# Warming products, the order of two GpSimd products and the places of weight loads in a fused attention and mixture-of-experts kernel

## The chip, the cores and the metric

The kernel runs on one core of one Trainium2 chip. The metric is the device time of one execution in microseconds (us); the time before the change is 430.35 us, the median of three runs (429.88 to 430.53). The engines are called TensorE (PE in the profile; PEld is its loading of weights), VectorE (DVE), ScalarE (ACT), GpSimd (POOL) and SyncE (SP, which here only issues transfers). "L351" is line 351 of the kernel before.

## The reference

Three stages run one after the other on 2 sequences of 768 tokens, all in fp32.

```python
for t in range(S):                       # 1: attention with a decaying state, 8 heads of 64
    state = gamma * state + outer(k[:, :, t], v[:, :, t])
    y[:, :, t] = scale * q[:, :, t] @ state
# 2: every token goes to one of 8 experts
e = argmax(x @ w_gate), or the expert of the token before, where sigmoid(x @ w_local) >= 0.5
out = softmax(x @ w_gate)[e] * (relu(x @ w1[e]) @ w2[e])         # 512 -> 1024 -> 512
# 3: a gated layer
h = relu(x @ w_in); gate = sigmoid(conv over 3 tokens of h); out = (h * gate) @ w_out
```

The weights of the third stage arrive as 64-bit floats, which the kernel decodes itself.

## The kernel before, in words

**The attention** is cut into 12 tiles of 128 tokens. A loop over i = 0 to 11 does tile i's second half and tile i+1's first half, so that the engines overlap. All instructions go into their engine's queue in the order in which the code writes them, and each engine works in that order; there is no scheduler.

- `a_S(i)` (L344): 16 products k by q on TensorE (L351), then VectorE masks them into A (L357, two instructions).
- `a_Z(i)` (L360): 16 products of q with the state carried over (L367).
- `a_AV(i)` (L371): 16 products of v with A (L379), the first eight on heads 0 to 3 and the others on heads 4 to 7; then ScalarE copies the result to xT (L384).
- `a_U(i)` (L387): 16 products that add k by v to the state (L397), and ScalarE's copy Z of it (L399).
- `a_X(i)` (L401): 8 products that turn xT into rows and give the gate's logits (L407); ScalarE copies the rows (L417) and stores them to DRAM (`a_store`, L410).
- `a_scale_q(i, engine)` (L324): q times a table of decays (L330). On GpSimd a one-element memset comes first (L328). It overwrites an element of the tile before, so it waits for that tile's products `a_S`.
- `a_scale_v(i)` (L332): v times its decays, heads 4 to 7 by one GpSimd instruction (L337), heads 0 to 3 by four on ScalarE (L340).
- `a_table(c)` (L318): ScalarE makes the tables of decays, one in each of the first steps.

The loop's step i issues `a_Z(i)`, the load of q and k for tile i+3, `a_X(i-1)`, `a_AV(i)`, `a_U(i)`, the load of k and v for tile i+3, `a_S(i+1)`, then `a_scale_q(i+2)` on GpSimd and `a_scale_v(i+1)`. Between these stand the pieces of the routing (`route`, L444, a generator advanced by `part`): after tiles 3, 6, 9, 11 and 12 a group of tiles gets its experts, its counts and its slots, in short VectorE instructions with small TensorE products between them. In step 8 `first_gather` (L590) reads the first expert's first 128 slots out of the state's PSUM bank (L594, L595) before `a_U(8)` may write that bank again, and GpSimd gathers those rows.

**Weights.** Each expert has 8 pieces of 512 KB (four of w1, four of w2), numbered over all experts in their order of use; I call them unit 0, unit 1, and so on. `load_unit` (L152) issues the next one on SP, into one of four buffers. `split_first` (L168) makes a unit's high part on ScalarE (L174), `split_second` (L178) its low part on VectorE (L183), which frees the buffer and then, unless told not to, loads another unit. Products use high and low parts in three passes. `LOADS` says how many loads stand at the end of each step of the attention, `SPLIT_STEPS` in which steps a `split_first` stands. Every step has a `split_second` without a load after `a_AV`. `dec_load` (L239) loads one 512 KB piece of the third stage's 64-bit weights, into one of two buffers; `DEC_STEP` says in which step the first two stand.

**After the loop** come `first_T` (the gathered first rows transposed and split, L599), `a_X(11)`, `logits(11)`, `a_store(11)`, the last groups of the routing, and then `moe` (L603). There, expert 0's first 128 rows (`alone`, L629, products L652 and L671) run between the last pieces of the routing; when the slots are known (`permi`, L768) GpSimd gathers the other rows (L611). `overflow` (L821) is a branch that is not taken with these data; its end stands in the queues of all engines. Behind it the decoding of the first 64-bit pieces (`decode`, L198) and expert 0's second 128 rows follow, then the six experts 1 to 6 (L707, L739), the last expert, and the third stage.

**The start** (L1085 to L1111): SP issues the loads of tiles 0 to 2, ScalarE's queue those of the tables. `keep_warm(10)` (L293) issues ten products on a zeroed tile `x_last` before the first work arrives, and ScalarE's first copy makes the engine load its activation table.

Of the kernel before, what the change touches and what calls it, by code (L numbers as in the profile page):

```python
# [41 lines left out]
Z_LT_HALF = -1.5 * 2.0 ** -23  # L42

WBUFS = 10
DEC_STEP = 10
SPLIT_STEPS = (4, 5, 6, 7, 8, 9)
LOADS = {2: 1, 3: 1, 4: 1, 5: 1, 7: 1, 8: 1, 9: 1, 10: 2, 11: 1}


def _float_of(bits):  # L50
# [49 lines left out]
def tile_kernel(ctx: ExitStack, tc: tile.TileContext, consts, qk, kv, w1, w2, w_in, conv_w, w_out, out):  # L100
# [138 lines left out]
    def dec_load(queue=nc.sync):  # L239
        u = dnx["load"]  # L240
        if u >= len(dec_src):
            return
        dnx["load"] += 1
        t = dp.tile([P, 2 * DM], I32, name="draw", tag="draw", bufs=2)
        queue.dma_start(out=t, in_=dec_src[u].bitcast(I32))
        dec_raw[u] = t
# [77 lines left out]
    def a_scale_q(i, engine, a=slice(0, 2)):  # L324
        if i >= NT:
            return
        if engine is nc.gpsimd:
            engine.memset(qk_t[i - 1][0:1, 0, 1, 0, 0:1], 0.0)  # L328
        t = qk_t[i][:, a, 0].rearrange("p a c t -> p a (c t)")
        engine.tensor_tensor(out=t, in0=t, in1=tabs[i % NC].rearrange("p (a n) -> p a n", a=2)[:, a], op=ALU.mult)  # L330
# [13 lines left out]
    def a_S(i, ms=(0, 1)):  # L344

        t = qk_t[i]
        for m in ms:
            for half in range(2):
                for j in range(2):
                    o = (2 * m + half) * P  # L350
                    nc.tensor.matmul(sc2[j][:, o:o + P], lhsT=t[HALF[j], m, 1, half, :], rhs=t[HALF[j], m, 0, half, :],  # L351
                                     start=True, stop=True)
        if ms[-1] == 0:
            return
        A_t[i] = [at.tile([P, NP, P], F32, name=f"A{j}", tag=f"A{j}", bufs=1) for j in range(2)]
        for j in range(2):
            nc.vector.tensor_tensor(out=A_t[i][j], in0=sc2[j].rearrange("p (a t) -> p a t", a=NP),  # L357
                                    in1=cv("mask").unsqueeze(1).to_broadcast([P, NP, P]), op=ALU.mult)
# [159 lines left out]
    def part(i):  # L518
        if i in rts:
            next(rts[i], None)  # L520
# [82 lines left out]
    def moe(mo):  # L603
# [158 lines left out]
        part(g3)  # L762
        next(first)
        part(g4)
        next(first)
        next(first)
        part(g4)
# [315 lines left out]
    with tc.manual_schedule():  # L1083
        a_load_qk(0, 2)
        for half in range(2):  # L1085
            n = slice(half * n0 // 2, (half + 1) * n0 // 2)
            nc.scalar.dma_start(out=tabs[0][:, n], in_=consts[:, n])
        n1 = off["ident"][0]
        nc.scalar.dma_start(out=C[:, 0:n1 - n0], in_=consts[:, n0:n1])
        nc.scalar.dma_start(out=C[:, n1 - n0:], in_=consts[:, n1:])  # L1090
        nc.scalar.dma_start(out=craw, in_=conv_w.bitcast(I32))
        a_load_kv(0, (1, 0))
        a_load_qk(1)
        a_load_kv(1)
        a_load_qk(2)
        a_load_kv(2)
        nc.vector.memset(x_last, 0.0)
        nc.scalar.copy(x_last[:, 0, 1:2], x_last[:, 0, 0:1])
        keep_warm(10)
        nc.vector.memset(small_zero, 0.0)  # L1100
        nc.gpsimd.memset(ones, 1.0)
        sloti = x0.bitcast(I32)[:, 0:CAP]
        nc.gpsimd.iota(sloti, pattern=[[1, CAP]], base=1, channel_multiplier=0)
        nc.gpsimd.tensor_copy(slot1, sloti)
        for half in range(2):
            a_scale_q(0, nc.vector, slice(half, half + 1))
            a_S(0, (half,))
        a_scale_v(0)
        a_table(1)
        a_scale_q(1, nc.vector)  # L1110
        nc.sync.dma_start(out=scr[0:1, :], in_=x_last[0:1].rearrange("p a t -> p (a t)"))  # L1111
        for i in range(NT):
            if i == 0:
                gate = C[:, n_wg:n_wg + KD * (E + 1)].rearrange("p (k e) -> p k e", k=KD)
                for odd in range(2):
                    o = (E + 1) * odd
                    nc.gpsimd.tensor_copy(xw[:, odd::2, o:o + P], ident.unsqueeze(1).to_broadcast([P, KD // 2, P]))
                    o = P if odd == 0 else 0
                    nc.gpsimd.tensor_copy(xw[:, odd::2, o:o + E + 1], gate[:, odd::2, :])
                nc.gpsimd.tensor_copy(tri, cv("mask"))  # L1120
                nc.gpsimd.tensor_copy(base, cv("base"))
                nc.gpsimd.tensor_copy(sel, ident[:, P - 1:P].to_broadcast([P, P]))
            ends = {b: g for g, (a, b) in enumerate(GROUPS)}
            last_tile = i == NT - 1
            fresh, due, late = (ends.get(i - n) for n in range(3))
            a_Z(i)
            a_load_qk(i + 3)
            part(due)
            if i:
                a_X(i - 1)  # L1130
                logits(i - 1)
                a_store(i - 1)
            if fresh is not None:
                rts[fresh] = route(fresh)
                part(fresh)
            a_AV(i)
            part(due)
            part(late)
            if i == FIRST + 2:
                first_gather()  # L1140
            split_second(nc.vector, False)
            a_U(i)
            if i + 2 < NC:
                a_table(i + 2)
            a_load_kv(i + 3)
            if not last_tile:
                a_S(i + 1)
                a_scale_q(i + 2, nc.gpsimd)
                a_scale_v(i + 1)
                part(due)  # L1150
            if i == 2:
                for _ in decode(craw, cw.rearrange("p a f -> p (a f)")):
                    pass
            for _ in range(LOADS.get(i, 0)):
                load_unit()
            if i == 1:
                spare = scr[YROW + CAP:YROW + (E - 1) * CAP, :].rearrange("(e r) d -> r e d", e=E - 2)[0:OFF]
                nc.gpsimd.dma_start(out=spare, in_=x_last[0:OFF].rearrange("p a t -> p (a t)").unsqueeze(1).to_broadcast(
                    [OFF, E - 2, DM]))
            if i == DEC_STEP:  # L1160
                dec_load()
                dec_load()
            if i in SPLIT_STEPS:
                split_first()
        first_T()
        a_X(NT - 1)
        logits(NT - 1)
        a_store(NT - 1)
        part(len(GROUPS) - 2)
        rts[len(GROUPS) - 1] = route(len(GROUPS) - 1)  # L1170
        part(len(GROUPS) - 1)
        att.close()
        with ExitStack() as c2:
            mo = c2.enter_context(tc.tile_pool(name="mo", bufs=1))
            moe(mo)
        dst.close()
        with ExitStack() as c3:
            fo = c3.enter_context(tc.tile_pool(name="fo", bufs=1))
            moe2(fo)
# [39 lines left out]
```

## Time and profile before

| what | us |
|---|---|
| median of 3 runs | 430.35 |
| the profiled execution, its own time | 430.57 |
| its span on the core (first to last instruction) | 428.8 |
| TensorE busy, share of the span | 394.6 (92%) |
| VectorE, ScalarE, GpSimd busy | 285.7, 250.9, 114.3 |

The span is what the profile's rows cover; 1.8 us of the execution's own time lie around it. A row of the timeline gives the start, the busy time, the engine, the line, the operation, the tiles written and read, and, in brackets, how long the engine had been idle and what released it. Busy shares are means over stages that have different limits, so the views by stretch and by wait are read stage by stage.

### The profile page before, as it was taken

Reading aid. Unit: us, or ns where it says so; the run is one execution under the profiler, and the core shown is the slowest. Engines: PE = TensorE matmul, PEld = TensorE weight load, DVE = VectorE, ACT = ScalarE, POOL = GpSimd, SP = SyncE. Lnnn points to the kernel's source line nnn. Section 1 sums busy time; section 2 is a strip of 40 time slices with the busy share of each in tenths; the row PEclk is TensorE's granted clock in tenths of the full one; section 3 lists DMA queues with packets and bytes.
Section 4 is the critical chain, followed back from the end, with each engine's and each line's share of the span. In section 5 each row is a group of like instructions: output and inputs, shape, how many; then the busy total and the mean of one; then the engine's idle time right before and its main releaser. Section 6 shows DMA issues by size and latency. Waiting matters only on the chain.

```text
span 428.8 us, 7360 instructions
## 1 busy us (share of the span) xinstructions
PE 394.6 (92%) x2772; PEld 340.3 (79%) x2772; DVE 285.7 (67%) x540; ACT 250.9 (59%) x489; POOL 114.3 (27%) x109
## 2 busy tenths in 40 slices
PE   5989898949999999999999949779999999999996
PEld 2778776637989898988989828559988989998986
DVE  1457877766797999887778764676990734992250
ACT  3777654627475766566756531657875635982441
POOL 3343450334005044554644442715000000000000
PEclk9999999997999999999999987999999999999999
DMA  7999995376869797888886140324101001001001
GB/s 265 305 318 354 383 326 209 110 240 240 300 213 300 216 311 277 303 281 273 289 266 224 53 141 0 99 74 125 48 0 75 1 26 50 2 0 49 26 0 73
DMA packets 28231, 73.37 MB, mean 171 GB/s; under 512 B 3025, under 2 KB 3793, under 8 KB 28194
## 3 DMA queue, kind: packets, MB, share of 16 engines
q1 hardware_dynamic: 19506, 54.67, 37.2%
q10 hardware_dynamic: 6384, 10.68, 6.8%
q0 software_dynamic: 2304, 7.54, 5.9%
q8 instruction: 22, 0.36, 0.3%
q14 instruction: 15, 0.12, 0.1%
HBM read 62.39 MB, written 10.49 MB: 170 GB/s over the span
## 4 chain that ended last, share of the span: by engine, by line
PE 64%; DVE 5%; ACT 3%; issue 2%; DMA 2%; POOL 2%; ACTq 0%; POOLq 0%; DVEq 0%
PE c L739 15%; PE c L1031 14%; PE b L979 9%; PE b L707 8%; PE rt L979 4%; PE state L707 4%; PE rt L707 4%; PE a L583 1%; PE b L1031 1%; PE c L671 1%; DMA raw<-in_moe_w_dram 1%; DMA yg<-scr,posi 1%; PE a L936 1%; DVE ds L222 1%; DVE wlo L183 1%
## 5 line engine op out<-in xcount | busy, mean ns | idle before, releaser
L183 DVE TENSOR_TENSOR wlo<-raw,whi 128x1024 fp32r<-128x1024 f32 x64 | 81.2, 1282 | 23.4 <-ACT whi L174 22.0
L174 ACT CAST whi<-raw 128x1024 fp32r<-128x1024 f32 x64 | 66.8, 1054 | 39.3 <-PE c L739 22.1
L998 DVE SCALAR_TENSOR_TENSOR cs<-hs,cw,cs 128x384 f32<-128x384 f32 x64 | 39.6, 620 | 32.9 <-ACT cs L996 31.8
L227 POOL TENSOR_TENSOR dmf<-dmf,ds 128x512 f32<-128x512 f32 x12 | 23.2, 1934 | 90.6 <-DVE ds L225 60.1
L739 PE MATMUL c<-whi,hh 128*112 128x512 f32 x96 | 38.0, 396 | 0.0
L979 PE MATMUL b<-x,whi 128*128 128x386 f32 x168 | 35.8, 341 | 1.9 <-ACT x L946 1.6
L739 PE MATMUL c<-wlo,hh 128*112 128x512 f32 x96 | 37.5, 390 | 0.0
L1031 PE MATMUL c<-whi,gh 128*128 128x512 f32 x88 | 35.0, 398 | 0.0
L1031 PE MATMUL c<-whi,gl 128*128 128x512 f32 x88 | 34.8, 395 | 0.0
L1031 PE MATMUL c<-wlo,gh 128*128 128x512 f32 x88 | 34.7, 394 | 0.0
L979 PEld LDWEIGHTS b<-x,whi 128*128 128x128 f32 x168 | 29.5, 189 | 3.3 <-ACT x L946 2.1
L739 PE MATMUL c<-whi,hl 128*112 128x512 f32 x96 | 29.6, 390 | 0.0
L707 PE MATMUL b<-xsh,whi 128*128 128x240 f32 x96 | 26.5, 276 | 0.0
L707 PE MATMUL b<-xsl,whi 128*128 128x240 f32 x96 | 26.5, 276 | 0.0
L707 PE MATMUL b<-xsh,wlo 128*128 128x240 f32 x96 | 26.3, 274 | 0.0
L611 POOL DMA_INDIRECT xg<-scr,permi x15 | 18.4, 1227 | 25.8 <-DVE nbi L542 18.8
L357 DVE TENSOR_TENSOR A<-b,C 128x512 f32<-128x512 f32 x24 | 15.5, 686 | 14.3 <-PE b L351 14.3
L228 POOL TENSOR_TENSOR wdec<-dmf 128x512 f32<-128x512 f32 x12 | 22.5, 1871 | 0.9
L1002 ACT ACTIVATE sg<-cs 128x384 f32<-128x384 f32 x32 | 16.7, 522 | 8.4 <-DVE gl L1008 8.0
L739 PEld LDWEIGHTS c<-whi,hl 128*112 128x112 f32 x96 | 17.4, 181 | 4.5
L739 PEld LDWEIGHTS c<-whi,hh 128*112 128x112 f32 x96 | 17.4, 181 | 4.3
L739 PEld LDWEIGHTS c<-wlo,hh 128*112 128x112 f32 x96 | 17.4, 181 | 4.2
(228 smaller groups left out, 1025.9 us busy)
## 6 DMA issues: line engine op xcount, KB each, us to landing
raw<-in_moe_w_dram SPq DMA_DIRECT2D x64, 512.0 KB, 5.4
qk<-in_qk_dram SPq DMA_DIRECT2D x11, 512.0 KB
kv<-in_kv_dram SPq DMA_DIRECT2D x11, 512.0 KB, 6.8
draw<-in_moe_w_in_dram SPq DMA_DIRECT2D x8, 512.0 KB, 5.7
draw<-in_moe_w_out_dram SPq DMA_DIRECT2D x8, 512.0 KB, 5.4
scr<-xo ACTq DMA_DIRECT2D x11, 256.0 KB, 5.7
out_dram<-os ACTq DMA_DIRECT2D x11, 256.0 KB, 2.6
scr<-ys ACTq DMA_DIRECT2D x10, 256.0 KB
```

Source lines behind the costliest of these rows:

```text
L174: nc.scalar.copy(hi, raw[u])
L183: engine.tensor_tensor(out=lo, in0=t, in1=hi.bitcast(F32), op=ALU.subtract)
L227: nc.gpsimd.tensor_tensor(out=f, in0=f, in1=s.bitcast(F32), op=ALU.mult)
L228: nc.gpsimd.tensor_tensor(out=out, in0=f, in1=a.bitcast(F32), op=ALU.add)
L357: nc.vector.tensor_tensor(out=A_t[i][j], in0=sc2[j].rearrange("p (a t) -> p a t", a=NP), in1=cv("mask").unsqueeze(1).to_broadcast([P, NP, ...
L611: nc.gpsimd.indirect_dma_start(out=t, out_offset=None, in_=xrow, in_offset=bass.IndirectOffsetOnAxis(ap=permi[:, col:col + 1], axis=0))
L707: nc.tensor.matmul(o, lhsT=a[:, fs], rhs=b_[:, dt, OFF:], start=(dt == 0 and n == 0 and ft % 2 == 0), stop=(dt == KD - 1 and n == 2), skip ...
L739: nc.tensor.matmul(yp[t][0:P - o], lhsT=a[:, ft, t * P + o:(t + 1) * P], rhs=b_[:, ws], start=(ft == 0 and a is hh and b_ is wh), stop=(ft ...
L979: nc.tensor.matmul(pb[:, 0:WN], lhsT=split[u_in + dt][wi][:, fs], rhs=x_[dt // 2][:, dt % 2, :], start=(n == 0), stop=(n == 3 * KD - 1))
L998: nc.vector.scalar_tensor_tensor(out=cs, in0=tap[j], scalar=cw[:, j, ft:ft + 1], in1=cs, op0=ALU.mult, op1=ALU.add)
L1002: nc.scalar.activation(out=sg, in_=cs, func=AF.Sigmoid)
L1031: nc.tensor.matmul(ops[t][:, 0:n_], lhsT=a[:, ts_], rhs=b_[:, ws], start=(ft == 0 and n == 0), stop=(ft == KF - 1 and n == 2))
```

## The change

It does five things. The ten warming products read `x_last` after its memset alone: ScalarE's first copy, which loads the activation table, now works on another small tile and stands behind them. In the attention, GpSimd scales v of tile i+1 before it scales q of tile i+2. Unit loads stand in steps 1, 2, 4, 5, 8, 9, 10, 11 (units 0 to 7) instead of 2, 3, 4, 5, 7, 8, 9, 10, 10, 11 (units 0 to 9). The first two loads of 64-bit weights and unit 8's load follow behind the loop, instead of in step 10. High parts are made in steps 4, 5, 6, 7, 10 and once behind `a_store(11)` instead of in steps 4 to 9; the low part of that last unit (unit 5), with the next load (unit 9), stands among the last pieces of the routing in `moe`.

```diff
-DEC_STEP = 10
-SPLIT_STEPS = (4, 5, 6, 7, 8, 9)
-LOADS = {2: 1, 3: 1, 4: 1, 5: 1, 7: 1, 8: 1, 9: 1, 10: 2, 11: 1}
+SPLIT_STEPS = (4, 5, 6, 7, 10)
+LOADS = {1: 1, 2: 1, 4: 1, 5: 1, 8: 1, 9: 1, 10: 1, 11: 1}
...
         part(g3)
         next(first)
         part(g4)
+        split_second(nc.vector)
         next(first)
         next(first)
         part(g4)
...
         nc.vector.memset(x_last, 0.0)
-        nc.scalar.copy(x_last[:, 0, 1:2], x_last[:, 0, 0:1])
         keep_warm(10)
         nc.vector.memset(small_zero, 0.0)
+        nc.scalar.copy(small_zero[:, 1:2], small_zero[:, 0:1])
...
                 a_S(i + 1)
+                a_scale_v(i + 1)
                 a_scale_q(i + 2, nc.gpsimd)
-                a_scale_v(i + 1)
                 part(due)
...
-            if i == DEC_STEP:
-                dec_load()
-                dec_load()
             if i in SPLIT_STEPS:
                 split_first()
+        dec_load()
+        dec_load()
+        load_unit()
         first_T()
         a_X(NT - 1)
         logits(NT - 1)
         a_store(NT - 1)
+        split_first()
         part(len(GROUPS) - 2)
```

## Rows read from the trace of the kernel before

**Rows 1.** The page, part 1: busy us, share of the span, instructions.

```profile
PE 394.6 (92%) x2772; PEld 340.3 (79%) x2772; DVE 285.7 (67%) x540; ACT 250.9 (59%) x489; POOL 114.3 (27%) x109
```

**Rows 2.** Windows of the attention: stretch, length, busy per engine, granted clock, DMA share, GB/s.

```profile
14.00:26.00 12.00, 11.47 (x180) 9.45 (x178) 5.47 (x13) 9.49 (x34) 6.39 (x9) 1.00 0.89 276
26.00:48.00 22.00, 21.07 (x338) 17.93 (x338) 16.58 (x52) 16.55 (x52) 8.36 (x15) 1.00 0.99 365
```

**Rows 3.** Timeline of the start: memset, warming products, q's first product, first tile's a_S.

```profile
0.93 0.48 DVE L1097 MEMSET x_last<- 128x512 f32 x1 [0.93 <-PEq L1207]
...
4.66 4.45 PE L297 MATMUL state<-x_last 128*128 128x512 f16 x10 [4.66 <-ACT x_last L1098]
...
5.26 0.42 DVE L330 TENSOR_TENSOR qk<-qk,tq 128x256 f32<-128x256 f32 x1 [0.48 <-DMA tq<-in_consts_dram]
...
9.04 1.18 PE L351 MATMUL b<-qk 64*128 64x128 f32 x16
```

**Rows 4.** Timeline: tile 1's load of q and k, its scaling, its a_S.

```profile
4.72 0.43 SPq L306 DMA_DIRECT2D qk<-in_qk_dram  x1
...
11.46 0.68 DVE L330 TENSOR_TENSOR qk<-qk,wdec 128x512 f32<-128x512 f32 x1
...
12.86 1.16 PE L351 MATMUL b<-qk 64*128 64x128 f32 x16
```

**Rows 5.** The page, part 6: KB of each transfer, median us from issue to landing.

```profile
kv<-in_kv_dram SPq DMA_DIRECT2D x11, 512.0 KB, 6.8
```

**Rows 6.** TensorE's waits from 12 to 53 us: total us, times, longest.

```profile
PE a L379 <- POOL kv L337: 1.9, 5, 0.9
```

**Rows 7.** Timeline: products v by A and state, in step 1 and in step 9.

```profile
15.69 0.66 PE L379 MATMUL a<-A,kv 128*64 128x128 f32 x8
...
16.51 0.66 PE L379 MATMUL a<-A,kv 128*64 128x128 f32 x8 [0.16 <-POOL kv L337]
...
17.00 0.63 PE L397 MATMUL state<-kv 128*64 128x64 f32 x16
...
55.77 1.19 PE L379 MATMUL a<-A,kv 128*64 128x128 f32 x16
...
56.79 0.64 PE L397 MATMUL state<-kv 128*64 128x64 f32 x16
```

**Rows 8.** Timeline of step 2: ScalarE's half of v, the products that read it.

```profile
19.13 1.05 ACT L340 ACTIVATE kv<-kv,C 128x64 f32<-128x64 f32 x4
...
20.38 0.66 PE L379 MATMUL a<-A,kv 128*64 128x128 f32 x8
```

**Rows 9.** Timeline of step 8: GpSimd's q, a VectorE count, two TensorE groups.

```profile
49.02 1.26 POOL L330 TENSOR_TENSOR qk<-qk,wdec 128x512 f32<-128x512 f32 x1 [2.09 <-DMA qk<-in_qk_dram]
49.08 1.23 DVE L499 TENSOR_TENSOR cnt<-up,C 128x8 f16<-128x8 f32 x1
...
50.91 0.66 PE L379 MATMUL a<-A,kv 128*64 128x128 f32 x8 [0.93 <-POOL kv L337]
...
52.33 0.69 PE L397 MATMUL state<-kv 128*64 128x64 f32 x16 [0.52 <-DVE perm L595]
```

**Rows 10.** Timeline of steps 10 and 11: ScalarE's high part of unit 5, TensorE behind it.

```profile
62.22 1.04 ACT L174 CAST whi<-raw 128x1024 fp32r<-128x1024 f32 x1 [3.42 <-DMA raw<-in_moe_w_dram]
...
65.19 0.67 PE L367 MATMUL a<-qk,Z 64*64 64x128 f32 x16 [1.51 <-ACT Z L399]
```

**Rows 11.** The page, part 5: the low parts on VectorE.

```profile
L183 DVE TENSOR_TENSOR wlo<-raw,whi 128x1024 fp32r<-128x1024 f32 x64 | 81.2, 1282 | 23.4 <-ACT whi L174 22.0
```

**Rows 12.** Timeline behind the branch: ScalarE, GpSimd and TensorE resume.

```profile
90.76 0.67 ACT L216 ACTIVATE dmf<-draw 128x512 f32<-128x512 f32 x1 [4.35 <-DMA raw<-in_moe_w_dram]
90.81 1.28 POOL L227 TENSOR_TENSOR df<-df,ds 128x512 f32<-128x512 f32 x1 [6.54 <-remote]
...
97.25 1.11 PE L640 MATMUL a<-C,hr 128*128 128x128 f32 x4 [6.59 <-ACT hr L663]
```

**Rows 13.** Windows behind that wait, same columns as rows 2.

```profile
98.00:101.00 3.00, 3.00 (x9) 2.42 (x8) 2.84 (x3) 1.66 (x3) 1.97 (x3) 0.50 0.39 128
```

## The prediction, made before the changed kernel was run

> **What bounds the kernel now.** The page comes first: TensorE is busy for 92% of the span [rows 1], but that is an average over stages. The change touches the attention and the first products behind it, so the views that count are the windows, the waits of TensorE and the timeline of that stretch. Three things are to be seen there. First, the start: the warming products wait for ScalarE until 4.66 us, though the tile they read is zeroed at 1.41 us, and tile 0's `a_S` queues behind them until 9.04 us, though its q is scaled by 5.68 us [rows 3]. Second, from 26 to 48 us the DMA engines are busy at a share of 0.99, from 14 to 26 us at 0.89 [rows 2]: an earlier start helps only as far as transfers come earlier too. Third, TensorE stops on other engines: five times on GpSimd's half of v, 1.9 us in all [rows 6], and 1.51 us behind a ScalarE that had itself waited 3.42 us for a weight [rows 10].
>
> I sum against the profiled execution (430.57 us, span 428.8, so 1.8 around it); it lies 0.2 above the median of 430.35, and what is saved is taken off the median.
>
> **Warming products.** Ten take 4.45 us [rows 3]. Started at 1.5 instead of 4.66 they end near 6.0; q is ready at 5.68, so tile 0's `a_S` moves from 9.04 to about 6.0, 3.1 us. ScalarE's copy and the table load keep their place in its queue, and nothing else there waits for TensorE. Of the 3.1 us the next wait takes most. Tile 1's q and k are issued at 4.72 whatever the change does. Their landing has no row: it lies before 11.46, when VectorE scales them [rows 4], and, with the 6.8 us that such loads take in the median [rows 5], at 11.5; with one 512 KB piece fewer in front of it (at 365 GB/s [rows 2], 1.4 us) it would be 10.1, an estimate. I take 11.0, nearer to the row that uses them. Scaling (0.68) and 0.1 for the semaphore put tile 1's `a_S` at 11.8 instead of 12.86: **1.0 us**, with ends at 0.6 (landing 11.46) and 2.0 (10.1). TensorE is then idle for some 2 us before it.
>
> **v before q on GpSimd.** The memset in front of q waits for `a_S(i+1)`, and v stood behind both. In front, v's 0.6 us run while that product is still to come, and nobody waits for q earlier than a step later. In steps 1 to 3 the two halves of `a_AV` then run without the gap: `a_AV` to `a_U` is 1.31 us in step 1 and 1.02 in step 9, where nothing was missing [rows 7], so 0.29 each, 0.9 in all. What is late next is ScalarE's half of v: it ends at 20.18 and the first half of `a_AV(2)` starts at 20.38 [rows 8]. So I take 0.2 for each, 0.6. The other waits of the 1.9 us are step 4 and step 8. Step 8 has 0.93 [rows 9]; steps 1 to 3 have about 0.5 together (0.16 in the row of step 1), which leaves step 4 some 0.5, with the split halves joined 0.6. Steps 1 to 4: **1.2 us** (0.9 to 1.5).
>
> Step 8 is different. Its `a_U` waits for VectorE's `perm` (0.52 us), not for v. VectorE's chain to it holds an instruction on 128x8 elements that took 1.23 us beside GpSimd's q, which had waited 2.09 us for its transfer [rows 9]; both end at 50.3. With the steps earlier by then, VectorE gets past that instruction before q lands, or it meets the same q one instruction later. I take **0.6 us**, ends 0 and 1.0. By the Trainium skill, "SBUF — State Buffer", section "Who interferes with whom", VectorE and GpSimd lock each other out of a shared port for a whole instruction, and some forms of `tensor_scalar` take that port as well; by that rule the slot instructions that follow would be caught instead, the term would be 0 and the sum 0.6 us smaller. The 1.23 us fit the rule; no row shows the slot instructions beside GpSimd.
>
> **Weight loads.** The attention issued ten units and two 64-bit pieces, each of 512 KB; now eight units in the loop, then the pieces and unit 8, and unit 9 from the added `split_second`. On SP they stand behind the last k and v, past which nothing else waits; the issue of unit 8 waits for unit 4's low part (step 11), and behind it in that queue stand only later units. Four units precede tile 9's q and k as before, so those land no earlier by this; units 0 and 1 one step sooner only fill the 11% that the DMA engines have free before 26 us (1.3 us). I cost the moves at nothing. The cover is the time until the units are used, behind the attention. Where it is thin is unit 9, which now runs just ahead of the gathers of expert 0; if it runs beside them, its 512 KB at 365 GB/s [rows 2] are 1.4 us.
>
> **High and low parts.** Without a high part at the end of step 9, ScalarE no longer stands 3.42 us behind unit 5's landing; the unit needed at the end of step 10 (now unit 4) has by then had two steps. `a_Z(11)` then waits only for the copy Z: **1.5 us** (1.0 if the later high part, 1.04 us [rows 10], delays the row copies of step 11). Late next is TensorE itself. The low part of unit 4 moves to step 11, 1.28 us on VectorE [rows 11], of which about 1.0 falls in its wait for ScalarE's part of the first rows: -0.2. Unit 5's low part falls among the routing's last instructions, where VectorE waits for TensorE between short pieces: -0.1. If half of each lay bare, they would cost 1.2, which is my low end; 0.1 is the other.
>
> **The sum:** 1.0 + 1.2 + 0.6 + 1.5 - 0.3 = 4.0 us, 430.35 - 4.0 = 426.35, so **426.4**. The low ends give 0.6 + 0.9 + 0 + 1.0 - 1.2 = 1.3 us (429.0), the high ones 2.0 + 1.5 + 1.0 + 1.5 - 0.1 = 5.9 (424.4). One thing stays: behind the branch ScalarE and GpSimd resume at 90.8 and TensorE at 97.25 after 6.59 us [rows 12]. Its start and end both move with the routing, so it neither shrinks nor eats the gain.
>
> **The rivals.**
> - *Transfers decide.* If tile 9's load (2.09 us late [rows 9]) lands when it did, the start and the first steps give nothing beyond about 0.5 us, and 1.5 stays from ScalarE: 2.0 us, 428.4. For it: the share of 0.99. Against: loads are issued as buffers come free, and buffers come free earlier. Chance 0.15.
> - *The start counts in full.* Tile 1's load lands in time for all 3.1 us, 2.1 more: 424.3. For it: VectorE takes up tile 1's scaling only behind the mask, so the load may have lain there [rows 4]. Against: the median of such loads [rows 5]. Chance 0.09.
> - *The clock, slower than before.* The ten products ran 0.43 us apart, 512 columns each, which is the level of 1.2 GHz; tile 0's `a_S` came right behind them. Now about 2 us without a product follow soon after. A fall is seen once: after a stop of 6.59 us TensorE runs at a granted clock of 0.50 from 98 to 101 us [rows 12, 13], 1.2 of 2.4 GHz. If the level stays low in the first steps, each microsecond costs half of itself, since products fill these steps; 4.0 us are gone when it is low for 8 us, and low until 18 us (12 us) gives 430.35 - 4.0 + 6.0 = 432.3. Against: stops of 1.5 us [rows 10] left the level at 1.00. By the Trainium skill, "TensorE: Matmul & The Clock Gate", section "What's actually happening", the watch on activity runs freely and does not begin with the kernel, so the moment of the rise can differ from run to run; no row here shows two starts. Chance 0.06.
> - *The stop behind the branch grows.* Unit 9 beside the gathers makes it 1.4 us longer: 427.8. Chance 0.04.
> - *It does nothing*, because another queue takes each wait's place within its step: 430.35. Chance 0.04.
>
> **How the numbers follow.** The forecast (425.2 to 427.7) has 0.62. The range is from 424.3 to 429.0: it takes in the ends of the sum, the transfers and the longer stop, and leaves out the slow clock, no change and the edges of the others, about 0.18. This kernel's runs agree within 0.2%, 0.86 us, which is what a measurement tells from no change. Faster by more than that: 0.62 + 0.15 + 0.09 + 0.04, less 0.01 for the edge of the transfers' case, 0.89. Same: 0.05. Slower: 0.06.
>
> **What would show it.** Right: warming from 1.5 us, tile 0's `a_S` near 6.0, tile 1's near 11.8, a TensorE gap before it; no wait of L379 on GpSimd; no wait of L174 for a transfer in step 9; the resume after the branch at about 93.2 instead of 97.25. Wrong: tile 9's `a_S` earlier by under 2 us (transfers), a granted clock of 0.50 between 6 and 20 us, or a stop behind the branch that isn't 6.6 us long, in which case the experts' start, not the attention, sets the result.

## The result: 6.2 us faster, and the profile after

The changed kernel took 423.90 us (423.49 to 424.96, 4 runs) beside 430.12 (429.51 to 430.53) of the kernel before: 6.2 us less, ratio 0.986 with a 95% interval of 0.9838 to 0.9883. In a second comparison, with more runs, it was 424.50 us (423.70 to 425.38, 6 runs) beside 428.95 (427.46 to 431.88, 12 runs): 4.5 us less, ratio 0.9888 (0.9857 to 0.9919). The forecast of 426.4, with 4.0 us of gain, had the sign and, but for the stop behind the branch, the mechanism; the time lies 0.4 us under its range.

The first profiled execution took 424.14 us, its span is 422.4 (before 428.8). In the changed kernel the lines quoted have numbers one lower (L350 is L351 of before). The page, part 1:

```profile
PE 395.0 (94%) x2772; PEld 342.0 (81%) x2772; DVE 286.3 (68%) x540; ACT 250.7 (59%) x489; POOL 116.7 (28%) x109
```

The engines are as busy as before [rows 1], within 0.6 us each and GpSimd 2.4 us more; only waits are gone. The account runs along TensorE's queue: one mark after the other, its start before and after, and what each stretch between two marks gave. The a_S(1), a_U(8), a_Z(11) of before can be read in [rows 4, 9, 10]. The others of the attention that stand in no row above or below are here, a_S(5), a_S(9), a_S(11) and the last a_X of before, then the three a_S of after:

```profile
33.15 1.16 PE L351 MATMUL b<-qk 64*128 64x128 f32 x16
...
52.94 1.16 PE L351 MATMUL b<-qk 64*128 64x128 f32 x16
...
62.32 1.16 PE L351 MATMUL b<-qk 64*128 64x128 f32 x16
...
68.58 1.20 PE L407 MATMUL c<-xw,x_last 128*128 128x137 f32 x8
```

```profile
29.44 1.16 PE L350 MATMUL b<-qk 64*128 64x128 f32 x16
...
48.12 1.16 PE L350 MATMUL b<-qk 64*128 64x128 f32 x16
...
57.40 1.16 PE L350 MATMUL b<-qk 64*128 64x128 f32 x16
```

| mark on TensorE | before | after | lead so far | this stretch gave | forecast |
|---|---|---|---|---|---|
| a_S(1) | 12.86 | 10.91 | 1.95 | start 1.95 | 1.0 |
| a_S(5) | 33.15 | 29.44 | 3.71 | steps 1 to 4: 1.76 | 1.2 |
| a_S(9) | 52.94 | 48.12 | 4.82 | steps 5 to 8: 1.11 (step 8 alone 1.16) | 0.6 |
| a_S(11) | 62.32 | 57.40 | 4.92 | 0.10 | 0 |
| a_Z(11) | 65.19 | 58.68 | 6.51 | ScalarE's stop: 1.58 | 1.5 |
| last a_X | 68.58 | 62.64 | 5.94 | -0.56 | -0.2 |
| resume behind the branch | 97.25 | 90.62 | 6.63 | routing -0.1, stop 0.8 | -0.1 and 0 |
| end of span | 428.8 | 422.4 | 6.4 | -0.2 | 0 |

**The start**, timeline of TensorE and of VectorE's scaling of tile 1:

```profile
1.47 4.45 PE L296 MATMUL state<-x_last 128*128 128x512 f16 x10 [1.47 <-DVE small_zero L1099]
...
5.85 1.22 PE L350 MATMUL b<-qk 64*128 64x128 f32 x16
...
10.16 0.69 DVE L329 TENSOR_TENSOR qk<-qk,wdec 128x512 f32<-128x512 f32 x1 [1.77 <-DMA qk<-in_qk_dram]
...
10.91 1.16 PE L350 MATMUL b<-qk 64*128 64x128 f32 x16 [1.12 <-DVE qk L329]
```

Tile 0's a_S starts 3.2 us earlier than in [rows 3], tile 1's 1.95 earlier than in [rows 4]. VectorE waits 1.77 us for tile 1's q and k to land, and TensorE 1.12 us for VectorE.

**TensorE's waits up to 72 us** (engine, what it runs, what it waits for; total us, times, longest):

```profile
PE b L350 <- DVE qk L329: 1.1, 1, 1.1
PE a L378 <- ACT kv L339: 0.8, 1, 0.8
PE a L366 <- ACT Z L398: 0.6, 1, 0.6
...
PE state L396 <- DVE perm L594: 0.5, 1, 0.5
```

The five waits on GpSimd's half of v [rows 6] are no longer among them, and of ScalarE's stop nothing is left: L366's wait stands at a_Z(4), where it was 0.43 us before. From 26 to 48 us the DMA engines are as full as in [rows 2] and move slightly more:

```profile
26.00:48.00 22.00, 21.41 (x340) 18.19 (x328) 17.42 (x53) 16.16 (x49) 10.11 (x14) 1.00 0.99 371
```

**Step 8**, timeline:

```profile
43.83 1.29 POOL L329 TENSOR_TENSOR qk<-qk,wdec 128x512 f32<-128x512 f32 x1 [0.56 <-DMA qk<-in_qk_dram]
...
45.42 0.17 DVE L498 TENSOR_TENSOR cnt<-up,C 128x8 f16<-128x8 f32 x1
...
47.51 0.69 PE L396 MATMUL state<-kv 128*64 128x64 f32 x16 [0.53 <-DVE perm L594]
```

GpSimd's q is over at 45.12, before VectorE's count begins; the count takes 0.17 us instead of 1.23 [rows 9], and from its start to a_U it is 2.09 us instead of 3.25.

**Steps 10 and 11**, timeline:

```profile
58.68 0.67 PE L366 MATMUL a<-qk,Z 64*64 64x128 f32 x16
58.76 1.04 ACT L173 CAST whi<-raw 128x1024 fp32r<-128x1024 f32 x1
...
61.09 0.68 ACT L416 COPY xo<-c 128x256 f32<-128x256 f32 x2 [1.28 <-DVE LG L440]
...
62.64 0.66 PE L406 MATMUL c<-xw,x_last 128*128 128x137 f32 x3 [0.39 <-ACT x_last L383]
```

The high part has no wait for a transfer (3.42 us in [rows 10]), and a_Z(11) starts without one. The last a_X waits in its place for ScalarE's copies, which wait for VectorE.

**The branch**, timeline of the third gather, the resume of ScalarE, GpSimd and TensorE:

```profile
77.00 1.43 POOL L610 DMA_INDIRECT xg<-scr,permi  x1 [0.30 <-issue]
...
84.12 0.67 ACT L215 ACTIVATE dmf<-draw 128x512 f32<-128x512 f32 x1 [3.49 <-DMA raw<-in_moe_w_dram]
84.17 1.29 POOL L226 TENSOR_TENSOR df<-df,ds 128x512 f32<-128x512 f32 x1 [5.75 <-PE rt L651]
...
90.62 1.11 PE L639 MATMUL a<-C,hr 128*128 128x128 f32 x4 [5.74 <-ACT hr L662]
```

From GpSimd's resume to TensorE's it is 6.45 us, before 6.44 [rows 12]: the decoding in between has not changed. What is shorter is the time up to GpSimd's resume.

### The profile page after: what moved, and what is told of

Read it like the earlier page. It is cut to its first block, busy times and chain, and to the rows that moved or that the text cites. A ratio compares the mean times of both kernels' runs of the same rounds, so it can differ in the third digit from the quotient of the medians.

```text
span 422.4 us, 7365 instructions
## 1 busy us (share of the span) xinstructions
PE 395.0 (94%) x2772; PEld 342.0 (81%) x2772; DVE 286.3 (68%) x540; ACT 250.7 (59%) x489; POOL 116.7 (28%) x109
## 4 chain that ended last, share of the span: by engine, by line
PE 64%; DVE 5%; issue 3%; DMA 3%; ACT 3%; POOL 2%; ACTq 0%; POOLq 0%; DVEq 0%
PE c L738 16%; PE c L1031 15%; PE b L979 8%; PE b L706 8%; PE rt L979 4%; PE state L706 4%; PE rt L706 4%; PE a L582 1%; PE c L670 1%; PE b L1031 1%; DMA raw<-in_moe_w_dram 1%; POOL yg L954 1%; DMA scr<-ys 1%; DVE cs L998 1%; DMA x_last<-scr,posi 1%
## 5 line engine op out<-in xcount | busy, mean ns | idle before, releaser
L182 DVE TENSOR_TENSOR wlo<-raw,whi 128x1024 fp32r<-128x1024 f32 x64 | 82.7, 1304 | 21.5 <-ACT whi L173 19.9
L610 POOL DMA_INDIRECT xg<-scr,permi x15 | 19.4, 1292 | 25.9 <-DVE nbi L541 18.9
L227 POOL TENSOR_TENSOR wdec<-dmf 128x512 f32<-128x512 f32 x12 | 22.5, 1872 | 0.9
```

Of the source, the lines that this page charges most:

```text
L182: engine.tensor_tensor(out=lo, in0=t, in1=hi.bitcast(F32), op=ALU.subtract)
L227: nc.gpsimd.tensor_tensor(out=out, in0=f, in1=a.bitcast(F32), op=ALU.add)
L610: nc.gpsimd.indirect_dma_start(out=t, out_offset=None, in_=xrow, in_offset=bass.IndirectOffsetOnAxis(ap=permi[:, col:col + 1], axis=0))
```

## The experiments

Theory: the start and steps 1 to 4 come from the warming products and from v's place, the rest from the loads and splits; the terms add. Rivals: one part carries most of it and the others are covered; or what scatters from run to run (the landing of transfers, the clock, the stop behind the branch) makes up a good part. Each profile is one execution, so stretches are compared first, and whole times only with their intervals.

### The parts one by one

**The warming change alone**, twice (kernel before, plus):

```diff
-        nc.scalar.copy(x_last[:, 0, 1:2], x_last[:, 0, 0:1])
+        nc.scalar.copy(small_zero[:, 1:2], small_zero[:, 0:1])
```

> The kernel before with the warming products alone moved. If the parts add up along one chain: tile 1's a_S near 10.9 instead of 12.86, the same pace behind it, about 1.9 us saved in the attention, 428.2 us. If transfers decide: tile 9's q comes as late as before, a_S of tile 9 stays near 52.9 and less than 0.5 us is saved, 429.7 us or more.

> The kernel before with the warming products alone moved, once more, for a second profile and more times: its first profile had the attention's end 3.3 us earlier while its median did not move. If the gap ahead of tile 1 lets the clock fall in most runs: a low stretch between 10 and 20 us, S of tile 2 near 18 to 19, attention no earlier than before. If transfers decide: no low stretch, but v waits behind a late q again in step 8 (0.9 us or more) and unit 5 stops ScalarE for 3 us or more.

Measured 429.44 us, ratio 1.0004 (0.9973 to 1.0035), and 427.60, ratio 0.9969 (0.9935 to 1.0002): neither can be told from no change. The lead at a_S(1) was 1.92 and 1.46 us, but the two profiles differ behind it. The first (427.01 us, the second shortest of its 12 times) has a_S(11) at 59.92 and a lead of 3.34 us at the last a_X (timeline):

```profile
61.84 0.67 PE L367 MATMUL a<-qk,Z 64*64 64x128 f32 x16 [0.56 <-ACT Z L399]
...
65.24 1.20 PE L407 MATMUL c<-xw,x_last 128*128 128x137 f32 x8
```

In the second (430.87 us, the second longest of its 10) the lead had grown to 2.5 us at a_S(11), at 59.80, and went between there and the last a_X:

```profile
60.76 1.04 ACT L174 CAST whi<-raw 128x1024 fp32r<-128x1024 f32 x1 [4.47 <-DMA raw<-in_moe_w_dram]
...
63.72 0.85 PE L367 MATMUL a<-qk,Z 64*64 64x128 f32 x16 [2.56 <-ACT Z L399]
64.51 2.19 PE L407 MATMUL c<-xw,xT 128*128 128x137 f32 x8
```

ScalarE's stop behind unit 5 is 2.47 us in the first and 4.47 us in the second, against 3.42 [rows 10]. With the old loads it is a draw: it adds 0.95 us to the lead of the first and takes 1.05 from the second's. In the second the clock fell too (eight products of 128x137 take 2.19 us, 1.21 elsewhere), and the last a_X came at 68.69, no earlier than the 68.58 of before. So the start's gain can arrive without the mended loads, and can be lost.

**v before q alone** (kernel before, plus):

```diff
-                a_scale_q(i + 2, nc.gpsimd)
                 a_scale_v(i + 1)
+                a_scale_q(i + 2, nc.gpsimd)
```

> The kernel before with v's product in front of q's on GpSimd alone. If the parts add up: 1.8 us in steps 1 to 4 and 1.1 in step 8, 2.9 us, 427.2 us. If step 8 depends on how early the steps before it are (VectorE caught behind GpSimd's q, which waits for its transfer): 1.8 us at most, 428.3 us. Tile 1's load of q and k, untouched here, lands at 10.9 to 11.1 if its landing in the changed kernel (near 10.1) came from the change, at 10 to 11 in a scattered way if it is chance.

Measured 426.82 us, ratio 0.9938 (0.9905 to 0.997). TensorE's timeline of step 1:

```profile
12.86 1.16 PE L351 MATMUL b<-qk 64*128 64x128 f32 x16
...
15.69 1.09 PE L379 MATMUL a<-A,kv 128*64 128x128 f32 x16
16.61 0.63 PE L397 MATMUL state<-kv 128*64 128x64 f32 x16
17.18 1.16 PE L351 MATMUL b<-qk 64*128 64x128 f32 x16
```

a_S(1) stands where it stood to the hundredth, the halves of a_AV run as one, and a_S to a_S is 4.32 us instead of 4.70. Steps 1 to 4 give 1.76 us, exactly the changed kernel's. Step 8 gave its 1.16 too, with the old loads.

**Loads and splits alone** (the changed kernel with the two diffs above undone: the old warming and q before v):

> The kernel before with the loads, the 64-bit pieces and the splits alone moved. If the parts add up: 1.6 us saved at a_Z(11), 0.5 to 0.7 lost at the last a_X, so about 1.0 saved, 429.1 us; with the shorter stop behind the branch (5.7 instead of 6.6 us), if that comes from these moves, 428.3 us. If the wait only changes its place: 430.1 us.

Measured 427.63 us, ratio 0.995 (0.9928 to 0.9972). ScalarE's stop gives 1.59, the last a_X takes 0.56 back, both as in the changed kernel. Step 8 again gives 1.16; GpSimd's q came earlier and VectorE's count met no lock (timeline):

```profile
46.85 1.46 POOL L329 TENSOR_TENSOR qk<-qk,wdec 128x512 f32<-128x512 f32 x1 [0.27 <-DMA qk<-in_qk_dram]
...
48.73 0.18 DVE L498 TENSOR_TENSOR cnt<-up,C 128x8 f16<-128x8 f32 x1
```

**The changed kernel with q before v:**

```diff
-                a_scale_v(i + 1)
                 a_scale_q(i + 2, nc.gpsimd)
+                a_scale_v(i + 1)
```

> The changed kernel with q in front of v again. If the parts add up: 2.9 us lost, 426.8 us. If an earlier start makes v wait longer behind a q whose transfer does not come earlier: step 8's wait of L379 on GpSimd grows from 0.9 to 2 us or more, 427.5 us or more.

Measured 427.38 us, ratio 0.9944 (0.9919 to 0.9969), against the changed kernel's 0.9888 and 0.986. From a_S(2) to a_S(5) it takes the 15.59 us of before, 14.22 after the change; step 8 still gave 1.0. Its profile also shows what the forecast's slow rival was about (TensorE's timeline, then the window with the granted clock ahead of the DMA share and GB/s):

```profile
9.20 0.69 PE L396 MATMUL state<-kv 128*64 128x64 f32 x16 [0.37 <-DMA kv<-in_kv_dram]
12.16 2.08 PE L350 MATMUL b<-qk 64*128 64x128 f32 x16 [2.27 <-DVE qk L329]
```

```profile
12.00:18.00 6.00, 5.84 (x46) 5.04 (x48) 1.73 (x5) 1.78 (x6) 1.93 (x3) 0.50 0.87 331
```

Tile 1's q and k landed late, TensorE rested for 2.27 us, and its clock was 0.50 (1.2 of 2.4 GHz) for the 6 us after. This profile was the slowest of the kernel's 12 executions (429.55), and three versions with v first show such a fall as well (below), so it is not put down to v's place.

**The two kernels again**, the changed one and the one before:

> The changed kernel, not edited, for its scatter beside that of the kernel before. If the clock falls in some runs in the gap ahead of tile 1's a_S (2 us or less of idle TensorE, as it did with q in front of v at 11.5 us), its times lie in two heaps some 3.5 us apart, 421 to 424 and 425 to 428. If the gap is too short with v first, one heap within 2 us. Tile 1's load of q and k lands somewhere between 10.0 and 11.4 us, whatever it did in the first profile.

> The kernel before, not edited, for a second profile: how far its own milestones scatter. If the first profile was typical: a_S(1) at 12.86, a_S(9) near 52.9, a_Z(11) near 65.2, resume behind the branch near 97.2, each within 0.5 us. If it was a late one: a_S(9) to 1.2 us earlier (VectorE not caught behind GpSimd) and a_Z(11) to 1.5 us earlier (no stop behind unit 5), as the profiles with one part of the change showed each of them.

The changed kernel's second result stands above. In its profile a_S(1) starts at 11.48 instead of 10.91, and from there every mark up to the branch lies 0.5 us later: up to there the start is what differs. The kernel before, against itself, had 429.73 us (427.36 to 431.83), ratio 1.0009 (0.9981 to 1.0036); in its profile ScalarE's stop costs TensorE 0.9 us less than in the first, and step 8 takes 6.30 us instead of 6.64. Between the second profiles of the two kernels the stretches of the table down to the resume give 1.78, 1.75, 0.79, 0.09, 0.65, -0.55 and 1.11 us: steps 1 to 4 and the loss at the last a_X repeat, the other large terms do not.

### The start

**A filled gap** between a_U(0) and a_S(1) of the changed kernel, the products on an idle bank:

```diff
+            if i == 0:
+                keep_warm(6, rtb)
             if not last_tile:
                 a_S(i + 1)
```

> The changed kernel with six more products of zeros, 1.3 us at the full clock, on an idle bank between a_U(0) and tile 1's a_S. If the gap costs nothing but its length: the same time or 0.3 us more. If the clock falls in it in some runs: those go, the median is 0.5 to 2 us lower than the changed kernel's beside it and the scatter is smaller.

Measured 425.02 us, ratio 0.9897 (0.9859 to 0.9934): no gain. There was no fall of the clock, which the changed kernel's profiles do not show either. a_S(1) starts at 11.78, right behind the sixth product, though tile 1 is scaled from 9.97: here the filling itself held it up by about 1 us.

**Tile 1's q and k ahead of a part of tile 0's k and v:**

```diff
-        a_load_kv(0, (1, 0))
+        a_load_kv(0, (1,))
         a_load_qk(1)
+        nc.sync.dma_start(out=kv_t[0].rearrange("p a h d -> p (a h d)")[:, 0:DM], in_=kv[0, :, 0:DM])
```

> The changed kernel, with tile 1's q and k issued ahead of the k half of tile 0's k and v. Disputed: what sets tile 1's a_S, at 10.91 and 11.48 us in the two profiles of the changed kernel. Theory: the landing of tile 1's q and k does. With 256 KB fewer in front of it (0.7 us at the 365 GB/s of rows 2) it is scaled from about 9.4 to 9.9 instead of 10.2 to 10.8, and a_S(1) starts at 10.2 to 10.8; tile 0's a_U may start later, but by less than it has room for. Some 0.6 us of the warming's 3 come through, the whole is 0.3 to 0.6 us faster than the changed kernel (ratio near 0.987 to 0.988), if nothing behind takes them back. Rival: VectorE's masking of tile 0 or another step of tile 0 sets it; then a_S(1) stays between 10.9 and 11.8 and a wait for k at a_U(0) may make it later.

Measured 424.27 us, ratio 0.9875 (0.9834 to 0.9916). VectorE's and TensorE's timeline:

```profile
8.67 0.69 DVE L329 TENSOR_TENSOR qk<-qk,wdec 128x512 f32<-128x512 f32 x1 [0.21 <-ACT wdec L320]
...
10.37 0.69 PE L396 MATMUL state<-kv 128*64 128x64 f32 x16 [0.98 <-DMA kv<-in_kv_dram]
10.98 1.16 PE L350 MATMUL b<-qk 64*128 64x128 f32 x16
```

Tile 1 is scaled 1.5 us earlier and VectorE no longer waits for a transfer, so the landing of q and k did set a_S(1). But now a_U(0) waits for k, which moved behind, and a_S(1) follows it at 10.98. The expected 10.2 to 10.8 did not come: in TensorE's order both tile 0's k and tile 1's q and k are needed before a_S(1), and together they land no sooner in either order. Step 8 gave 0.65 us here and 0.62 with the filled gap, not 1.16: GpSimd's q came 2.3 us after a_S(8), 1.2 in the changed kernel, and held VectorE's count (timeline):

```profile
44.96 1.27 POOL L329 TENSOR_TENSOR qk<-qk,wdec 128x512 f32<-128x512 f32 x1 [1.63 <-DMA qk<-in_qk_dram]
...
45.48 0.78 DVE L498 TENSOR_TENSOR cnt<-up,C 128x8 f16<-128x8 f32 x1
```

**One warming product instead of ten** (`keep_warm(1)` in the changed kernel):

> The changed kernel with one warming product instead of ten. It prices a cold clock at the start, the thing that the runs with a clock fall in the gap before tile 1's a_S lost. Theory: tile 0's a_S still starts at 5.85 to 6 us, since q's scaling sets it; the granted clock is then low in tile 0's products and, if the gap before a_S(1) counts as rest, in tile 1's too; each microsecond of products at the low level costs up to half a microsecond where products fill the stretch: from a_S(1) to a_S(2) 5 to 6.5 us instead of 4.31. a_S(2) at 16 to 18 us instead of 15.2 to 15.8, the whole 0.5 to 2 us slower than the changed kernel, ratio 0.990 to 0.994. Rival: the start does not matter at all, because transfers set a_S(5) anyway; then a_S(5) stays within 0.5 us of 29.4 to 30.0 and the ratio stays at 0.986 to 0.990.

Measured 426.08 us (424.67 to 427.40, 8 runs), ratio 0.9902 (0.9865 to 0.9939). TensorE's timeline, and the window of its first a_S:

```profile
4.97 2.12 PE L350 MATMUL b<-qk 64*128 64x128 f32 x16 [2.88 <-DVE qk L329]
...
11.51 2.08 PE L350 MATMUL b<-qk 64*128 64x128 f32 x16 [0.64 <-DVE qk L329]
...
17.83 1.16 PE L350 MATMUL b<-qk 64*128 64x128 f32 x16
```

```profile
4.00:7.00 3.00, 2.03 (x16) 1.83 (x16) 0.85 (x2) 1.16 (x4) 0.44 (x1) 1.00 1.01 350
```

Tile 0's a_S takes 2.12 us instead of 1.22, but its slack hides that: a_S(1) at 11.51 is the 11.48 of the changed kernel's second profile. Step 1 then takes 6.32 us instead of 4.31, and the 2.0 us are still there at a_S(5), 32.03 against 30.00. In the profile the rival falls: a clock at its upper level at a_S(1) is worth 2 us, before it nothing. The whole time points the same way but does not show it: the ratio is 0.9902 beside 0.9888, and the intervals overlap.

### The loads and the splits

**Unit 4's high part at the end of step 9 again**, and **the old steps of the first eight loads**, each in the changed kernel:

> The changed kernel with unit 4's high part at the end of step 9 instead of step 10. If ScalarE's stop behind that unit's landing was the whole of the 1.6 us at a_Z(11): unit 4 is issued near 48.8 and lands near 54.3 at the earliest, ScalarE reaches it near 53.9, so the stop is back with 0.5 to 3 us, and a_Z(11) waits 0 to 1.5 us; in exchange the last a_X is not delayed by 0.56 us: between 0.6 us faster and 1.0 us slower. If another wait made the 1.6 us: it stays away, 0.6 us faster.

> The changed kernel with its eight units loaded in the steps of before (2, 3, 4, 5, 7, 8, 9, 10), splits as changed. With unit 4's high part at the end of step 9 ScalarE did not stop, so the split's place alone does not explain the 1.6 us. If the place of the loads does (no unit in step 7, so a shorter queue ahead of what ScalarE takes up): in this kernel unit 4 is issued in step 7 and taken up at the end of step 10, three steps later, so the stop stays away too, and what shows is GpSimd's q of tile 9 waiting longer for its transfer, without cost; 0 to 0.5 us slower. If either the splits or the loads alone suffice: no difference in a_Z(11). If step 8's term needs the new loads: a_S(9) 1.1 us later.

```diff
-SPLIT_STEPS = (4, 5, 6, 7, 10)
+SPLIT_STEPS = (4, 5, 6, 7, 9)
```

```diff
-LOADS = {1: 1, 2: 1, 4: 1, 5: 1, 8: 1, 9: 1, 10: 1, 11: 1}
+LOADS = {2: 1, 3: 1, 4: 1, 5: 1, 7: 1, 8: 1, 9: 1, 10: 1}
```

Measured 425.34 us, ratio 0.9916 (0.9883 to 0.9948), and 425.48, ratio 0.9892 (0.9828 to 0.9956). In both, ScalarE has no wait for a transfer and a_Z(11) follows a_S(11) as in the changed kernel: either move suffices (the high part of step 8 is gone in both). In both the last a_X still comes 0.56 us late, with unit 4's high and low part out of the way in the first, so that loss is neither part's. It is VectorE's chain: two masks, a count, the slots, then the copy LG that ScalarE's rows wait for (the 1.28 us above). The masks wait for a_S(11), so the chain was there before as well, under ScalarE's stop.

### The stop behind the branch

**The branch's end later** in expert 0's first 128 rows, and **the first two decodings moved into its second 128 rows**, each in the changed kernel:

```diff
-            if n == 3:
-                overflow(mo)
...
+            elif n == 8:
+                overflow(mo)
```

```diff
-            if n == 5:
-                dec_first()
-            elif n == 6:
-                dec_first(mo)
-            elif n == 7:
-                dec_second()
         for n, _ in enumerate(alone(0, 1, True)):
+            if n in (8, 12):
+                dec_first()
+            elif n in (10, 14):
+                dec_second()
```

> The changed kernel with the branch (overflow) five pieces of expert 0 later, behind the decoding of the second 64-bit piece. If the stop of 5.7 us comes from engines that wait at the branch's end for the third gather to land: ScalarE and VectorE decode before it, the stop shrinks to 2 us or less and the clock does not fall, 4 to 6 us faster. If the decoding itself holds ScalarE: the stop stays over 4 us, 1 us faster at most.

> The changed kernel with the decoding of the first two 64-bit pieces moved from in front of expert 0's second 128 rows into its second half. If the stop behind the branch is the sum of the wait for the third gather and of the decoding behind it on ScalarE and VectorE: ScalarE then resumes as before near 84 us, with nothing to decode first, the stop falls from 5.7 to below 2 us, the clock does not fall, 4 to 7 us faster, near 418 to 420. If only the wait for the gather counts: 1 us at most.

The first: 425.96 us, ratio 0.9906 (0.9869 to 0.9943); the stop is 5.5 us and only changes its place. The second: 426.64 us, ratio 0.9924 (0.9878 to 0.997). TensorE's timeline:

```profile
89.49 0.66 PE L639 MATMUL a<-C,hr 128*128 128x128 f32 x4 [1.76 <-ACT hr L662]
...
101.88 0.38 PE L706 MATMUL b<-xsl,whi 128*128 128x240 f32 x1 [2.73 <-DVE xsl L585]
```

The stop shrinks to 1.76 us and the six experts begin at 98.76, 2.5 us sooner than in the changed kernel though the last a_X was 2.8 later: so the decoding is what fills the stop once the engines resume. But expert 1's products then wait 2.73 us for VectorE, the experts' second products 3.0 us more, and the third stage starts at 284.76, 5.3 us later than after the change. The work has to stand somewhere, and the stop was its cheapest place among the two tried.

No version tried beats the changed kernel beyond its interval. In whole times v's place alone gave 0.62%, the loads and splits 0.50%, the warming products nothing or 0.31%: 1.1 to 1.4% together, and the change 1.12 and 1.40%. So the parts add, as far as the intervals tell, and none carries it alone.

## Why the forecast had the mechanism right and the sizes too small

**Warming products (1.0 us forecast, 1.95 and 1.38 measured).** Right: from 1.47 us on, tile 0's a_S near 6.0, a wait for tile 1's transfer that takes the rest, a gap before a_S(1). The term of the sum that failed is the landing, taken at 11.0, "nearer to the row that uses them". VectorE took the tile up at 10.16 and 10.73, between that and the estimate of 10.1. The row of before could not settle it, and one number for it was too sharp: over the ten profiles with this start and tile 1's load in its old place, VectorE took the tile up between 9.97 and 11.49 us. In the nine of them without a filled gap a_S(1) starts at 11.56 in the mean (10.91 to 12.24), in the four with the old start at 12.87 (12.50 to 13.26). That is a gain of 1.3 us; the 1.95 of the first profile was a lucky draw.

**v before q, steps 1 to 4 (1.2 forecast, 1.76 measured).** The step that failed is the 0.2 a step. It was cut from 0.29 for ScalarE's half of v as the next thing late, which never was late. And the 0.29 was measured against step 9, "where nothing was missing": with v first, step 9 takes 4.31 us instead of 4.41, so it had lost 0.1 to v itself (the 0.10 at a_S(11) in the table). Steps 1 to 4 gave 0.39, 0.39, 0.43 and 0.56 (0.6 forecast for the last). This term is the firmest: from a_S(2) to a_S(5) it took 14.20 to 14.22 us in all ten profiles with v first, and 15.58 to 15.60 in all six with q first.

**Step 8 (0.6 forecast, 1.16 measured).** The place was right, and in the first pair the whole lock went. The Trainium skill, "SBUF — State Buffer", section "Who interferes with whom", has the two engines lock each other out for a whole instruction; the trace agrees with that (1.23 us beside q, 0.17 alone). What decides the size is when tile 9's q lands. The count is due 2.8 us after a_S(8) in every profile. In five profiles (both of before, the first with the warming alone, the filled gap, tile 1's load moved) GpSimd took q up 2.15 to 2.72 us after a_S(8), and the count took 0.66 to 1.23 us, ending 0.02 to 0.03 us behind q each time. In the other eleven it took q up 0.7 to 1.6 us after, and the count took 0.17 to 0.18, with q first in the changed kernel 0.41. The forecast had VectorE past the count before q lands, or caught by q one instruction later. Neither came: q was over before the count began, or the same count was held for less. Its other reading, that the slot instructions would be caught and the term be 0, did not come true in any profile: they took 0.68 us in all. That no row shows them beside GpSimd was wrong too: in the trace of before they run from 50.65 us, beside GpSimd's v, which ends at 50.85, and take the same 0.68. Nor does the gain belong to one part: it came with v's place alone, with the loads alone, and in the second profile with the warming alone, but not in the first.

**ScalarE's stop (1.5 forecast, 1.58 measured) and the low parts (-0.3 forecast, -0.66 measured).** The mechanism of the first is right, and it belongs to the loads or the splits alike. Its size is that of one profile: a_S(11) to a_Z(11) took 1.92 to 3.92 us in the five profiles with the old loads and splits, and 1.28 to 1.29 in the other eleven, so what was removed is 0.6 to 2.6 us. The 0.1 that the routing lost is not shown to be unit 5's low part: from the last a_X to the stop behind the branch TensorE took 22.08 to 22.22 us in the profiles without it and 22.05 to 22.63 in those with it and the branch in its place. The other 0.56 was put down to the low part of unit 4 and is VectorE's chain, late next once the stop is gone.

**The branch (0 forecast, 0.8 measured).** "It neither shrinks nor eats the gain" failed. From the third gather to GpSimd's resume it is 7.98 us before (82.83 to 90.81), 7.17 after, and 6.71 in the changed kernel's second profile; the decoding behind it takes 6.4 to 6.5 us each time. No part owns the difference: with the warming alone it was 7.77 in one profile and 6.58 in the other, and with v's place alone, and the old loads, 6.78:

```profile
79.70 1.43 POOL L611 DMA_INDIRECT xg<-scr,permi  x1 [0.30 <-issue]
86.48 1.30 POOL L227 TENSOR_TENSOR df<-df,ds 128x512 f32<-128x512 f32 x1 [5.35 <-PE b L652]
```

TensorE's stop was 5.2 to 6.6 us in the profiles in which the decoding stood in its old place, 6.59 and 6.53 in the two of before, 6.31 and 5.18 with the warming alone. Seven of these traces tell when the third gather landed: 5.8 to 7.1 us after its issue began, and in each GpSimd resumes 0.82 to 0.83 us behind that landing. So the time that differs is the gather's, and the branch's end seems to hold GpSimd until it has landed; an experiment without that hold was not made, and why the landing differs stays open. A stop that is not 6.6 us long was among the forecast's own signs of being wrong. So 0.8 of the first profile's 6.4 us may be luck, as some 0.6 of its start are, which fits the smaller gain of the second comparison, 4.5 us, close to the forecast's 4.0. Even so the changed kernel's own time, 424.5, lies near the range's low end.

**The rivals.** Transfers do not decide the whole: a_S(9) came 4.8 us earlier, though a landing still sets what step 8 gives. The start does not count in full: 1.95 of tile 0's 3.2 us come through. The slow clock did not show in the changed kernel's two profiles, but in four variants with the same ten products it did. It cost three of them 1.55 us in step 1 and the one with q first 2.4 (a_S to a_S 7.12 us instead of 4.70), not 6: the level was low for 3.4 us in the three and 6.8 in the other, where the forecast's case had 12. What the changed kernel's other executions did there is not seen. The forecast saw one fall in the trace of before; there is a second, to 0.50 from 254.9 to 261.7 us, behind a stop of 2.47 us and inside another of 3.38.

## What to carry to other kernels

Costing each removed wait by what is late next gave the right terms; what hangs on no transfer (steps 1 to 4, the chain before the last a_X) repeated from profile to profile, and the size of steps 1 to 4 was missed by a cut that the row gave no reason for and by a reference step that was not clean. A time that one execution shows for a landing, or for a stop that hangs on one (a_S(1), step 8, ScalarE's stop, the branch), is a draw and belongs in the range, not in the sum. A lead won early can be lost at the next transfer that does not move with it: with the warming change alone one profile kept 3.3 us at the last a_X, the other nothing, and the whole time showed nothing certain.

## What the runs showed of the hardware

**The clock at the start depends on more than the gap.** With the split at step 9 and with the old load steps, a_S(1) starts at 11.71 and 11.70 us after waits of 1.63 and 1.68 us. TensorE's windows of the two, in this order:

```profile
12.00:15.00 3.00, 3.00 (x48) 2.57 (x48) 1.61 (x4) 1.59 (x6) 2.08 (x4) 1.00 1.03 421
```

```profile
12.00:15.00 3.00, 3.00 (x34) 2.45 (x31) 1.29 (x2) 1.06 (x4) 2.09 (x4) 0.50 1.03 420
```

One kept 2.4 GHz, the other ran at 1.2 and lost 1.55 us by a_S(2). The trace's record of the clock begins with its rise: at 6.61 us in the first and at 5.18 in the second, for the same ten products from 1.47 us. By the Trainium skill, "TensorE: Matmul & The Clock Gate", section "What's actually happening", the watch on activity runs freely, so the moment differs from run to run; these two starts agree with that. Over the eleven profiles with that start the rise came between 4.65 and 7.41 us. Of the five in which it came by 5.44, four fell, after waits of 1.68 to 2.69 us (the fifth waited 1.51); of the six in which it came at 6.00 or later none did, but none of them waited over 1.63 us, so wait and moment are not told apart by these alone. Behind the branch the clock fell in the profiles with a stop of over 5 us, and not where the stop was 1.76 us, nor in that version's wait of 2.73 us in front of expert 1.

**The granted clock before the first rise can't be read from the column.** With one warming product it says 1.00 from 4 to 7 us, while 16 products that take 1.22 us elsewhere took 2.12; there the durations tell the level.

**VectorE's decoding is slowed beside GpSimd.** After the resume in the changed kernel, L219 took 1.37 us while GpSimd's L227 ran (85.54 to 86.86):

```profile
85.54 1.32 POOL L227 TENSOR_TENSOR wdec<-df,dmag 128x512 f32<-128x512 f32 x1
85.78 1.37 DVE L219 TENSOR_SCALAR dmf<-dmf 128x512 int32<-128x512 int32 x1
```

With the decodings moved, GpSimd ran nothing between 81.3 and 100.26, and the same line took 0.43 us, as it did in the 14 executions of it in the changed kernel's trace with nothing on GpSimd beside them, 11 of them on the tile of the slow one:

```profile
98.14 0.43 DVE L219 TENSOR_SCALAR dmag<-dmag 128x512 int32<-128x512 int32 x1
```

The 0.9 us between them lie in the 6.45 from GpSimd's resume to TensorE's; an order that keeps GpSimd's decoding out of VectorE's way there was not tried.
